# Two weight products by 20 products of blocks instead of 22 in halves

## The chip, the cores and the metric

The kernel runs on one core of one Trainium2 chip. Its time is the device time of one execution in microseconds (us). A core has five engines that run side by side, each with its own instruction stream worked off in order: TensorE (PE, matmuls; PEld is its weight load), VectorE (DVE), ScalarE (ACT), GpSimd (POOL) and SyncE (SP, which here issues the DMAs). They wait for each other through semaphores. Matmuls read SBUF and write PSUM, of which this kernel uses eight banks of 128 x 512 float32; GpSimd works on SBUF alone here.

## The reference

A linear-attention block (RWKV5), with 4 batches, 8 heads, 768 steps and head size 48, feeds a multiplicative feed-forward block on 3072 tokens. The weights `w1`, `w2`, `w3` and `w_out` reach the kernel as float64; all is worked on in float32.

```python
for t in range(S):
    cur = np.einsum('bhd,bhe->bhde', u[None] * kt, vt)
    y[:, :, t] = np.einsum('bhd,bhde->bhe', rt, state + cur)
    state = w[None, :, :, None] * state + np.einsum('bhd,bhe->bhde', kt, vt)
x = np.ascontiguousarray(y.transpose(0, 2, 1, 3)).reshape(B * S, H * D)   # 3072 x 384
a = x @ w1                     # 384 x 1024
b = x @ w2                     # 384 x 1024
out = (a * b @ w3) @ w_out     # 1024 x 1024, 1024 x 384
```

## The kernel before

**Chunks and units.** Time is cut into six chunks (c = 0 to 5) of 128 steps. A unit n is one batch of one chunk, 24 in all; the four units of a chunk give 512 tokens, which stand as `xT[c]`: 128 partitions x 3 blocks of the 384 features x 512 tokens.

**The stages.** First the float64 weights are fetched in 8 + 8 + 16 pieces and converted in place to float32 (words W, M, N or p, H, L, Q; p is a GpSimd instruction, line 396). `w3` is folded with `w_out` into `w34`, 1024 x 384: G turns a row block on VectorE, F multiplies it on TensorE (16 records, line 427), X takes it. F.7 is the last one. Beside this and behind it run the attention of the units (U, A, S, V and others on TensorE; k, d, e, f, x, i, j, m, Y on VectorE; yt turns a unit's output and yx puts it in `xT`), the two products a and b of every chunk, and the products P of a*b with `w34`. Chunk 0 takes a and b by plain matmuls on 512 columns (line 759). The P of a chunk is a seven-product scheme of 2x2 blocks (line 817), two rows of tokens (m = 0, 1) x 7 products x 8 records, with sums s (lines 799, 802) ahead and E (lines 837 to 851) and stores D behind.

**Chunks 1 to 5, a and b.** This is what changes. `product_half` (words pa and pb, lines 912 to 927) takes 2/3 of the features by a seven-product scheme on 2x2 blocks and the last third by plain matmuls: for each weight (a: `w1`, b: `w2`), chunk and half of the output columns (g = 0, 1) there are 8 words, which make 22 matmuls of 128 x 128 weights with 256 token columns. The chip runs a float32 matmul here as two records. They accumulate in four banks: A and F of pool `psF` (4 banks, shared with P, yt and the attention's outputs), B and C of pool `psT` (2 banks, taken once by `ps`, line 897, and kept). `gather_half` (words ga and gb, lines 929 to 953) copies the partial sums between the products with ScalarE, adds with VectorE, and for b multiplies into the tile `abt` of a. The sums of the weights (wa, wb, line 885) and of the tokens (xs, lines 892 to 895) are made by VectorE, the weights' once, the tokens' once in each chunk.

**The order.** Every engine works off its instructions in the order of the list `ORDER`: the function `listed` reads a word such as pa.2.1.4 and calls `product_half("a", 2, 1, 4)`, which issues its instructions on their engines. Nothing reorders them later; semaphores for the data and for the release of buffers are put in for each word. The word Z issues filler matmuls (`busy_array`, line 955). kr, v and W issue loads, y and z the scratch transfers and D the stores, all on SP's queue.

**Buffers that the change touches.** `krin` (the k and r of a unit) has 3 tiles, `abt` 9 of 128 x 2 x 512, the scratch tag `sa` 3 of 128 x 512; the sums s take tiles of their own and, for the other chunks, parts of the weight loads' `raw` tiles.

Of the kernel before, what the change touches and what calls it, by code (L numbers as in the profile page):

```python
# [23 lines left out]
v.1 kr.2 uw k.1 vs.0 ka.0 Z.4.0 T.1 kb.0 T.0 t.1 v.2 U.0 N.0 t.0 R.0 kr.3 ku.0 i.0 j.0 vp.1 U.1 R.1 i.1 r.0 j.1 r.1  # L24
A.0 kr.4 Au.0 k.2 M.0 S.1 S.0 ku.1 m.0 vp.2 R.2 T.2 mo.0 W.1 t.2 H.0 A.1 W.2 r.2 Au.1 fe.0 k.3 L.0 V.0 kr.5 Y.0 m.1
R.3 T.3 ku.2 mo.1 U.2 Q.0 A.2 t.3 Au.2 i.2 r.3 v.3 m.2 yt.0 M.1 mo.2 yx.0 fe.1 ku.3 k.4 Z.3.0 A.3 W.3 V.1 p.2 N.1 R.4
Y.1 v.4 H.1 T.4 M.2 S.2 j.2 kr.6 yt.1 L.1 Au.3 fe.2 H.2 V.2 yx.1 vp.3 Y.2 m.3 a.0.0.0 mo.3 L.2 W.4 yt.2 Q.1 M.3 U.3
W.5 i.3 p.3 t.4 Q.2 b.0.0.0 r.4 v.5 yx.2 k.5 ku.4 a.0.1.0 ub x.5 vp.4 c.0.0.0 A.4 H.3 c.0.1.0 S.3 y.5 ps fe.3 M.4 p.4
u.0.0.0 j.3 L.3 d.5 V.3 W.6 Q.3 M.5 U.4 v.6 Au.4 H.4 p.5 Y.3 kr.8 m.4 yt.3 L.4 b.0.1.0 mo.4 yx.3 i.4 vp.5 a.0.0.1 H.5
W.7 cz.1 a.0.3.2 L.5 Q.4 W.8 M.6 Q.5 p.6 c.0.0.1 vs.6 k.6 b.0.2.2 c.0.3.2 z.5 x.6 H.6 u.0.1.0 M.7 p.7 b.0.4.2 e.5 f.5  # L30
M.8 y.6 h.5 kr.7 L.6 j.4 H.7 S.4 W.9 U.5 L.7 fe.4 Q.6 V.4 l.5 Q.7 p.8 W.10 cz.0 Y.4 A.5 H.8 a.0.2.2 m.5 L.8 W.11 i.5
j.5 M.9 p.9 Q.8 b.0.3.2 k.7 c.0.2.2 z.6 H.9 M.10 p.10 u.0.2.2 L.9 Q.9 a.0.4.2 H.10 u.0.3.2 L.10 W.12 p.11 M.11 Q.10
x.7 a.0.1.1 c.0.4.2 H.11 W.13 L.11 u.0.4.2 U.6 l.6 Q.11 a.0.6.2 k.8 W.14 c.0.1.1 d.6 M.12 p.12 e.6 f.6 v.7 H.12
b.0.0.1 y.7 c.0.6.2 d.7 kr.9 p.13 M.13 e.7 L.12 b.0.1.1 f.7 H.13 Q.12 A.6 M.14 u.0.0.1 p.14 b.0.6.2 L.13 W.15 i.6 vs.7
Q.13 H.14 j.6 L.14 W.16 Q.14 a.0.5.2 u.0.6.2 m.6 W.17 x.8 M.15 p.15 u.0.1.1 a.0.7.2 c.0.5.2 d.8 e.8 z.7 H.15 M.16 p.16
b.0.5.2 L.15 c.0.7.2 Q.15 H.16 W.18 M.17 p.17 L.16 yt.4 Q.16 S.5 yx.4 U.7 g.6 fe.5 W.19 H.17 V.5 b.0.7.2 G.0.0 Y.5
L.17 v.8 u.0.5.2 W.20 l.7 Q.17 p.18 G.0.1 yt.5 M.18 A.7 u.0.7.2 g.7 F.0 i.7 y.8 kr.10 p.19 H.18 j.7 M.19 m.7 L.18 H.19
yx.5 W.21 M.20 Q.18 G.1.0 L.19 p.20 Q.19 vs.8 W.22 U.8 G.1.1 X.0 S.6 H.20 F.1 k.9 L.20 z.8 Q.20 G.2.0 M.21 p.21 x.9
fe.6 H.21 W.23 M.22 p.22 k.10 L.21 V.6 Q.21 X.1 S.7 H.22 W.24 l.8 fe.7 G.2.1 V.7 L.22 Y.7 A.8 W.25 Q.22 yt.7 F.2 G.3.0
yx.7 M.23 p.23 Y.6 i.8 y.9 v.9 j.8 kr.11 M.24 p.24 H.23 m.8 L.23 Q.23 M.25 G.3.1 p.25 yt.6 W.26 X.2 pa.1.0.0 H.24 yx.6  # L40
f.8 L.24 F.3 H.25 ga.1.0.0 Q.24 L.25 W.27 Q.25 g.8 G.4.0 G.4.1 W.28 vs.9 x.10 p.26 M.26 d.9 F.4 z.9 e.9 X.3 f.9 H.26
M.27 p.27 d.10 L.26 e.10 g.9 Q.26 H.27 W.29 p.28 G.5.0 f.10 L.27 Q.27 P.0.0.0 M.28 W.30 X.4 G.5.1 l.9 P.0.1.0 H.28
d.11 L.28 y.10 F.5 e.11 W.31 Q.28 M.29 p.29 G.6.0 f.11 kr.12 H.29 M.30 p.30 v.10 L.29 Q.29 H.30 pa.1.0.1 z.10 X.5
G.6.1 p.31 L.30 M.31 Q.30 F.6 ga.1.0.5 G.7.0 xs.1.0 E.0.0.0 xs.1.1 xs.1.2 kr.13 vs.10 H.31 s.0.1.0 L.31 Q.31 s.0.1.1
# [63 lines left out]
def kernel(  # L108
# [980 lines left out]
```

## Time and profile before

| | |
|---|---|
| median of 3 runs | 500.32 us (497.06, 500.32, 500.47) |
| the profiled execution | 498.53 us |
| its span, first to last instruction | 496.7 us |
| mean granted TensorE clock | 0.988 of full speed |
| F.7 starts, ends | 145.0, 150.4 us |
| last matmul ends | about 490.8 us |
| products of chunks 1 to 5 (lines 922, 926) | 560 + 320 records of 128x256 |

The profile is one execution. A busy time is the time in which an engine had work; matmuls overlap, so the printed duration of one is longer than the step to the next. The slices cut the span in 40 equal parts, with the busy share in tenths. The chain is followed back from the last instruction: at each step to what released it. In a list of instructions the columns are the start, the duration, the engine, the line, what is written and read, its shape and the count; in brackets stands the idle time ahead of it and who ended it. In the table of stages each engine's busy time is followed by its count of instructions, and the last three columns are the granted clock, the share of the DMA engines and GB/s.

### The profile page before, as it was taken

How to read it: one execution, taken by the hardware profiler on the slowest of the kernel's cores; microseconds unless marked ns; L12 is line 12 of the kernel's file. 1: busy time of each engine (PE TensorE's matmuls, PEld its weight loads, DVE VectorE, ACT ScalarE, POOL GpSimd, SP SyncE). 2: the span in 40 equal slices, each digit the busy share in tenths (PEclk: the TensorE clock that was granted, in tenths of full speed). 3: DMA queues.
4: the chain of work that ended last, by engine and by line, in shares of the span. 5: the costliest groups of instructions: out<-in, count | busy, mean ns of one | idle time of the engine just before them, and what ended most of it. 6: DMA issues, size and time to landing. Idle time of an engine off the chain costs nothing.

```text
span 496.7 us, 12176 instructions
## 1 busy us (share of the span) xinstructions
PE 476.6 (96%) x5070; PEld 395.0 (80%) x5070; DVE 328.5 (66%) x647; ACT 197.2 (40%) x454; POOL 62.1 (13%) x57
## 2 busy tenths in 40 slices
PE   8889699999999999999999999999999999999995
PEld 7776445566768988998788898898998889888895
DVE  5879789899999266648694993677472536325152
ACT  3866444857722114008715472332253232122200
POOL 3147354454400000000000000000000000000000
PEclk9989889999999999999999999999999999999999
DMA  8988859899932004325623551034150000100002
GB/s 177 251 230 252 201 163 232 210 215 246 224 72 63 2 16 129 96 65 154 154 78 95 132 127 34 18 112 145 48 148 13 1 3 12 54 1 0 1 1 69
DMA packets 100479, 52.72 MB, mean 106 GB/s; under 512 B 79296, under 2 KB 89792, under 8 KB 100416
## 3 DMA queue, kind: packets, MB, share of 16 engines
q1 hardware_dynamic: 99792, 51.86, 40.5%
q8 instruction: 42, 0.69, 0.6%
q14 instruction: 21, 0.17, 0.1%
q10 hardware_dynamic: 624, 0.00, 0.1%
HBM read 39.65 MB, written 12.19 MB: 104 GB/s over the span
## 4 chain that ended last, share of the span: by engine, by line
PE 82%; DVE 7%; issue 2%; ACT 2%; POOL 2%; DMA 1%; SPq 1%; ACTq 0%; POOLq 0%; DVEq 0%
PE ps_accB L922 10%; PE ps_w L427 6%; PE ps_Ab L922 4%; PE ps_accC L926 3%; PE ps_accC L922 3%; PE ps_a L759 3%; PE ps_s4b L817 3%; PE ps_accB L926 3%; PE ps_a12b L817 3%; PE ps_Aa L922 3%; PE ps_a11b L817 3%; PE ps_s3t L817 3%; PE ps_s1t L817 3%; PE ps_s2t L817 3%; PE ps_a22t L817 3%; PE ps_b L759 3%
## 5 line engine op out<-in xcount | busy, mean ns | idle before, releaser
L396 POOL TENSOR_SCALAR t<-raw 128x512 f32<-128x512 f32 (+2 forms) x30 | 52.4, 1747 | 64.0 <-PE ps_a L570 9.0
L922 PE MATMUL ps_accB<-sumw,w 128*128 128x256 f32 x160 | 45.9, 389 | 0.0
L427 PE MATMUL ps_w<-wo,w3T 128*128 128x384 f32 x128 | 42.7, 488 | 0.0
L427 PEld LDWEIGHTS ps_w<-wo,w3T 128*128 128x128 f32 x128 | 24.0, 190 | 15.5 <-issue 0.2
L471 ACT ACTIVATE ynat<-vnat,dg 128x48 f32<-128x48 f32 x144 | 34.4, 324 | 0.6 <-PE ps_x L729 0.4
L922 PEld LDWEIGHTS ps_accB<-sumw,w 128*128 128x128 f32 x160 | 28.9, 190 | 6.0 <-ACT u2a L939 1.1
L735 ACT COPY xT<-ps_x 128x384 f32<-128x384 f32 x24 | 11.5, 479 | 52.3 <-PE ps_x L729 52.3
L527 ACT COPY kT<-tt 128x1024 f32<-128x1024 f32 x19 | 19.8, 1043 | 24.8 <-PE ps_y L690 18.7
L405 ACT ACTIVATE t<-raw 128x512 uint32<-128x512 uint32 (+2 forms) x32 | 22.6, 706 | 13.4 <-DVE wo L401 5.2
L441 DVE TENSOR_TENSOR krs<-krin,pn_in 128x768 f32<-128x768 f32 (+1 forms) x25 | 23.5, 948 | 5.8 <-PE ps_a L563 4.1
L759 PE MATMUL ps_a<-xT,w 128*128 128x512 f32 (+1 forms) x60 | 24.4, 555 | 0.8 <-ACT xT L735 0.8
L926 PE MATMUL ps_accB<-xT,w 128*128 128x256 f32 x80 | 23.8, 379 | 0.0
L922 PE MATMUL ps_accC<-xT,sumw 128*128 128x256 f32 x80 | 23.8, 379 | 0.0
L926 PE MATMUL ps_accC<-xT,w 128*128 128x256 f32 x80 | 23.8, 379 | 0.0
L922 PE MATMUL ps_Ab<-xT,w 128*128 128x256 f32 x80 | 22.6, 384 | 0.4 <-ACT ps_accB L937 0.4
L759 PE MATMUL ps_b<-xT,w 128*128 128x512 f32 (+1 forms) x60 | 22.2, 512 | 0.5 <-DVE half L609 0.5
L922 PE MATMUL ps_Aa<-xT,w 128*128 128x256 f32 x80 | 22.3, 381 | 0.4 <-ACT ps_accB L937 0.4
L922 PE MATMUL ps_accB<-sumw,sumw 128*128 128x256 f32 x80 | 20.7, 382 | 0.0
L759 PEld LDWEIGHTS ps_a<-xT,w 128*128 128x128 f32 x60 | 11.9, 204 | 10.7 <-issue 8.8
L713 PE MATMUL ps_y<-vodd,AT 64*64 64x48 f32 x384 | 15.6, 222 | 4.4 <-DVE AT L702 3.4
L759 PEld LDWEIGHTS ps_b<-xT,w 128*128 128x128 f32 x60 | 11.1, 191 | 9.6 <-issue 7.9
L570 PE MATMUL ps_a<-kT 64*64 64x64 f32 x768 | 17.1, 226 | 1.6 <-ACT kT L527 0.8
(187 smaller groups left out, 1095.0 us busy)
## 6 DMA issues: line engine op xcount, KB each, us to landing
raw<-in_moe_w_dram SPq DMA_DIRECT2D x64, 128.0 KB, 3.4
scratch<-tr SPq DMA_DIRECT2D x19, 384.0 KB, 3.4
raw<-in_moe_w_dram SPq DMA_DIRECT2D x8, 768.0 KB, 6.2
tt<-scratch SPq DMA_DIRECT2D x38, 128.0 KB, 2.8
krin<-in_k_dram SPq DMA_DIRECT2D x24, 192.0 KB, 4.0
krin<-in_r_dram SPq DMA_DIRECT2D x24, 192.0 KB, 4.1
vnat<-in_v_dram SPq DMA_DIRECT2D x24, 192.0 KB, 3.9
raw<-in_moe_w_out_dram SPq DMA_DIRECT2D x32, 96.0 KB, 2.4
```

Source lines behind the costliest of these rows:

```text
L396: nc.gpsimd.tensor_scalar(part["t", i].bitcast(F32), words(i)[1].bitcast(F32), 0.0, None, ALU.mult)
L405: nc.scalar.activation(out=part["t", i], in_=words(i)[0], func=COPY, scale=2.0 ** -29)
L427: nc.tensor.matmul(ps, lhsT=w3T[j][:, kc, :], rhs=wo[kc], start=(kc == 0), stop=(kc == KF - 1))
L441: nc.vector.tensor_mul(krs[n % NS][:, which, :, :D], kr[:, which], pn[:, which, :, :D])
L471: nc.scalar.activation(out=ynat[n][:, h, :], in_=vnat[n % NV][:, h, :], func=COPY, scale=dg[n][:, h:h + 1])
L527: nc.scalar.copy(out=turned(n).rearrange("x g p (z t) -> x (g p) z t", t=Q), in_=tts.rearrange("x z e t -> x e z t"))
L570: nc.tensor.matmul(upper(n)[rows(a ^ i), i, p, :], lhsT=kT[n][rows(i), p, rows(a)], rhs=rT[n][rows(i), p, rows(a)], start=True, stop=True)
L713: nc.tensor.matmul(yt[n][i][rows(a), p, :], lhsT=AT[n][rows(at), i, p, :], rhs=values, start=not (c or a or p), stop=True, skip_group_chec ...
L759: nc.tensor.matmul(ps, lhsT=(w1 if x == "a" else w2)[:, z, q, js], rhs=xT[c][:, q, ts], start=(q == 0), stop=(q == KM - 1))
L817: nc.tensor.matmul(ps, lhsT=operand(c, j // 2, a)[:, j % 2, m * C:(m + 1) * C], rhs=w34[:, KH * (x == 1) + j, :DH] if x < 2 else made[b][: ...
L922: nc.tensor.matmul(ps, lhsT=quarter(w, g, i, x), rhs=(b11, b21, b22, t4, b12, t2, t3)[x], start=x in (0, 4) and i == 0, stop=True, skip_gr ...
L926: nc.tensor.matmul(ps, lhsT=wide_of[w][:, g + half * HZ, 2, i * P:(i + 1) * P], rhs=xT[c][:, 2, side * TH:(side + 1) * TH], start=False, s ...
```

## The change

For chunks 1 to 5 the scheme of a and b is replaced. The 384 features x 1024 columns of a weight are cut into 3 x 4 blocks, the 384 features x 512 tokens into 3 x 2, and the product is made by 20 products of one block or sum of blocks with another, each with two matmuls on 256 token columns (`product_of_blocks`, words pa.c.x and pb.c.x). Each is added to one of seven accumulators (`INTO`): number 1, 2 and 6 share the two banks of `psT`, number 0, 3, 4 and 7 take a bank of `psF`. `gather_blocks` (ga and gb) reads them out, in mid-accumulation too, with 7 copies on ScalarE (8 for a), 13 instructions on VectorE (14 for b), one addition on GpSimd, and for b seven products by the a side on GpSimd (on VectorE in chunk 5). The sums of the tokens are 3 on VectorE and 10 on GpSimd for each chunk; of the 18 sums of each weight all are on VectorE for `w1`, 5 on VectorE and 13 on GpSimd for `w2`. `krin` has 2 tiles instead of 3, `abt` 8 instead of 9, `sa` 4 instead of 3; the sums s all go to parts of the load tiles. `ps` is gone. The whole list `ORDER` is new; nine Z words with 34 filler matmuls stand in it, for two with 7 before. The counts of all other words are the same. Below, the removed functions are those printed above; of the list the start, the first units, the end of the fold and the head of chunk 5 are shown.

```diff
...
+v.1 v.2 W.1 uw ka.0 k.1 vs.0 Z.2.0 T.0 U.0 t.0 kb.0 R.1 kr.2 ku.0 N.0 R.0 i.0 j.0 r.0 Z.1.1 U.1 vp.1 M.0 kr.3 T.1 i.1
+vp.2 j.1 A.0 t.1 H.0 Au.0 r.1 S.0 ku.1 S.1 m.0 mo.0 W.2 L.0 fe.0 N.1 Z.3.0 A.1 M.1 W.3 Q.0 k.2 ub H.1 Z.6.0 R.2 kr.4
...
+a.0.0.0 M.4 fe.2 W.5 Q.2 p.4 c.0.1.0 V.2 d.5 c.0.0.0 e.5 b.0.0.0 Y.2 v.5 f.5 vp.4 H.4 yt.2 R.4 d.6 yx.2 b.0.1.0 e.6
+L.4 p.6 f.6 M.6 W.7 Q.4 T.4 Au.3 t.4 u.0.0.0 U.3 m.3 ku.4 p.5 i.3 mo.3 Z.1.0 S.3 r.4 j.3 M.5 Z.1.0 A.4 fe.3 k.5 V.3
+vp.5 Au.4 M.7 v.6 cz.1 kr.7 x.5 Y.3 H.5 y.5 H.6 L.5 Q.5 vs.6 Z.10.0 U.4 W.8 yt.3 L.6 m.4 p.7 yx.3 mo.4 W.9 Z.4.0
...
+vs.10 wa.0 wa.9 wa.12 G.7.1 wa.2 F.7 wa.10 X.6 wa.13 wa.14 wa.15 wa.5 wa.6 s.0.0.0 s.0.1.0 wa.1 wa.4 wa.7 wa.8 pa.1.18
+B.0 X.7 xs.1.5 pa.1.15 ga.1.0 xs.1.8 s.0.0.1 pb.1.15 ga.1.1 xs.1.6 ga.1.2 pa.1.2 xs.1.10 B.1 pa.1.8 xs.1.9 s.0.1.1
...
+pa.5.7 gb.4.23 gb.4.22 pb.4.12 Y.22 pb.4.9 gb.4.24 P.4.0.0 gb.4.25 gb.4.26 pb.4.19 E.4.0.0 gb.4.27 s.4.0.0 pb.5.7
+gb.4.28 yt.22 s.4.0.1 P.4.0.1 yx.22 s.4.1.0 xs.5.9 xs.5.3 pa.5.18 s.4.1.1 xs.5.7 s.4.1.3 pa.5.13 ga.5.0 xs.5.5 s.4.0.3
+pa.5.10 s.4.0.2 xs.5.2 P.4.0.2 s.4.1.2 xs.5.11 E.4.0.1 pa.5.15 xs.5.4 E.4.0.2 P.4.0.3 xs.5.6 ga.5.1 ga.5.2 xs.5.12
+pa.5.2 E.4.0.3 xs.5.8 pa.5.8 xs.5.10 pa.5.17 ga.5.4 ga.5.5 pa.5.3 ga.5.10 pa.5.14 ga.5.13 ga.5.7 pa.5.11 ga.5.6
+P.4.0.4 ga.5.8 ga.5.9 pa.5.4 E.4.0.4 ga.5.11 pa.5.20 ga.5.14 pa.5.6 P.4.0.5 ga.5.15 pa.5.5 E.4.0.6 E.4.0.5 P.4.0.6
+D.4.0.0 ga.5.17 pa.5.16 E.4.0.7 D.4.0.1 pb.5.17 ga.5.19 pa.5.1 ga.5.20 ga.5.21 pb.5.15 ga.5.23 pa.5.12 pa.5.9 ga.5.24
...
-    NIN, NV, NS = 3, 3, 2
+    NIN, NV, NS = 2, 3, 2
...
-                abt[c, g] = work.tile([P, 2, NT], F32, tag="abt", bufs=KF + 1, name=f"abt{c}_{g}")
+                abt[c, g] = work.tile([P, 2, NT], F32, tag="abt", bufs=KF, name=f"abt{c}_{g}")
...
-            factor["sa", c, j, part] = a = work.tile([P, NT], F32, tag="sa", bufs=3 if fast else 2, name=f"a{c}_{j}")[:, :ps.shape[1]]
+            factor["sa", c, j, part] = a = work.tile([P, NT], F32, tag="sa", bufs=4 if fast else 2, name=f"a{c}_{j}")[:, :ps.shape[1]]
...
+        split = lambda t: t[:, :NT].rearrange("p (g t) -> p g t", g=2)
+        spare = [split(t.bitcast(F32)[:, x * NT:(x + 1) * NT]) for t in raws for x in range(2 * RAW // NT)] \
+            + [split(t.rearrange("t g h d -> t (g h d)")) for t in (*krin, krs[0])]
...
+                n = 3 if (c, g) == (NCH - 1, 1) else (2 * c + g) % 3
+                s1, s2, s4 = spare[3 * n:3 * n + 3]
...
+                made[nm, c, m] = t = room().tile([P, DH], F32, tag=nm, bufs=1 if fast and nm == "m1" else 2, name=f"{nm}_{c}_{m}")
...
+        NZ = DF // STRIP
+        wide_of = {"a": w1, "b": w2}
+        def block(w, i):
+            return wide_of[w][:, i // KM, i % KM, :]
+        def sums_of_w(w, x):
+            if ("n", w) not in made:
+                tiles = [wide_pool.tile([P, DF], F32, tag="w3", bufs=4, name=f"sumw{2 * (w == 'b') + i}") for i in range(2)]
+                made["n", w] = [t[:, z * STRIP:(z + 1) * STRIP] for t in tiles for z in range(NZ)]
+            n = made["n", w]
+            a = [block(w, i) for i in range(NZ * KM)]
+            out, of, sign, by = ((n[0], a[0], "--", a[10]), (n[1], a[9], "++", a[10]), (n[7], a[0], "++", a[1]),
+                                 (a[1], a[1], "+-", a[10]), (a[9], a[0], "+-", a[9]), (n[4], a[8], "+-", a[11]),
+                                 (a[8], a[7], "+-", a[8]), (n[2], a[8], "++", a[11]), (a[0], a[0], "--", n[2]),
+                                 (n[3], a[6], "--", a[7]), (a[6], a[3], "--", n[3]), (n[4], n[4], "+-", a[6]),
+                                 (a[2], a[2], "+-", a[11]), (n[5], a[6], "+-", a[2]), (n[5], n[5], "+-", a[5]),
+                                 (a[5], a[4], "+-", a[5]), (n[6], a[5], "+-", a[2]), (n[7], n[7], "--", n[6]))[x]
+            if sign == "--":
+                nc.vector.scalar_tensor_tensor(out, of, -1.0, by, ALU.mult, ALU.subtract)
+            else:
+                engine = nc.gpsimd if w == "b" else nc.vector
+                (engine.tensor_add if sign == "++" else engine.tensor_sub)(out, of, by)
+        def wide_side(w, x):
+            n = made.get(("n", w)) or [None] * 8
+            a = lambda i: block(w, i)
+            return {1: n[0], 2: a(10), 3: n[3], 4: a(11), 5: a(8), 6: n[2], 7: n[4], 8: a(6), 9: n[1], 10: n[6], 11: n[5], 12: a(1),
+                    13: a(3), 14: a(7), 15: a(4), 16: a(0), 17: a(2), 18: a(5), 19: a(9), 20: n[7]}[x]
+        def tokens(c):
+            return [xT[c][:, q, x * TH:(x + 1) * TH] for q in range(KM) for x in range(2)]
+        V_AT = (16, 7, 15, 8, 6, 2, 14, 5, 10, 1)
+        def sum_of_tokens(i):
+            if ("v", i) not in made:
+                n = V_AT.index(i)
+                made["v", i] = (work if n < 5 else room()).tile([P, TH], F32, tag=f"x{'wr'[n > 4]}{n % 5}", bufs=1, name=f"x{'wr'[n > 4]}{n % 5}")
+            return made["v", i]
+        def sums_of_x(c, x):
+            b = tokens(c)
+            out, of, add, by = ((16, b[0], 0, b[2]), (7, 16, 0, b[4]), (15, b[3], 1, b[5]), (8, 7, 1, b[1]),
+                                (6, 7, 0, b[5]), (2, b[3], 0, b[1]), (14, 2, 0, 6), (b[0], b[0], 1, b[1]),
+                                (5, b[4], 1, b[5]), (10, b[2], 0, b[5]), (b[4], b[2], 1, b[4]), (b[3], b[2], 1, b[3]),
+                                (1, b[1], 1, b[2]))[x]
+            out, of, by = (sum_of_tokens(t) if isinstance(t, int) else t for t in (out, of, by))
+            engine = nc.vector if x in (0, 1, 3) else nc.gpsimd
+            (engine.tensor_add if add else engine.tensor_sub)(out, of, by)
+        def token_side(c, x):
+            b = tokens(c)
+            plain_or_shared = {18: b[5], 4: b[5], 13: b[1], 9: b[1], 20: b[2], 3: b[0], 19: b[0], 11: b[4], 12: b[3]}
+            return plain_or_shared[x] if x in plain_or_shared else sum_of_tokens(5 if x == 17 else x)
+        INTO = {1: (18, 10, 20, 12), 2: (13, 8, 3, 11), 6: (4, 6, 5, 16, 1, 9, 19), 3: (15,), 4: (7, 14), 0: (17,), 7: (2,)}
+        def product_of_blocks(w, c, x):
+            k = next(k for k, of in INTO.items() if x in of)
+            first = INTO[k][0] == x
+            if first:
+                made["B", w, c, k] = psT.tile([P, NT], F32, tag="t", name=f"ps_acc{k}{w}{c}") if k in (1, 2, 6) \
+                    else psF.tile([P, NT], F32, tag="f", name=f"ps_h{k}{w}{c}")
+            u, ps = wide_side(w, x), made["B", w, c, k]
+            for i in range(2):
+                nc.tensor.matmul(ps[:, i * TH:(i + 1) * TH], lhsT=u[:, i * P:(i + 1) * P], rhs=token_side(c, x),
+                                 start=first and i == 0, stop=True, skip_group_check=True)
+        def gather_blocks(w, c, x):
+            B = lambda k: made["B", w, c, k].rearrange("p (i t) -> p i t", i=2)
+            def out(k):
+                return pair_of(c, k // 2)[:, :, k % 2 * TH:(k % 2 + 1) * TH]
+            def part(k):
+                if w == "a":
+                    return out(k)
+                if ("T", c, k) not in made:
+                    made["T", c, k] = work.tile([P, NT], F32, tag="sa", bufs=4, name=f"T{k}b{c}").rearrange("p (i t) -> p i t", i=2)
+                return made["T", c, k]
+            copies = {0: (3, 1, -1.0), 4: (5, 2, 1.0), 5: (4, 4, 1.0), 8: (2, 2, 1.0), 10: (0, 0, 1.0), 13: (7, 7, 1.0), 19: (1, 6, 1.0)}
+            adds_to = {1: (3, 3), 2: (3, 2), 6: (5, 4), 7: (4, 2), 14: (7, 6), 15: (5, 6), 17: (4, 6), 26: (7, 6)}
+            takes = {9: (2, 1), 21: (0, 1), 23: (7, 6)}
+            by = {3: 3, 12: 2, 16: 5, 18: 4, 22: 0, 25: 1, 27: 7}
+            if x in copies:
+                k, of, scale = copies[x]
+                nc.scalar.activation(out=part(k), in_=B(of), func=COPY, scale=scale)
+            elif x in adds_to:
+                k, of = adds_to[x]
+                nc.vector.tensor_add(part(k), B(of), part(k))
+            elif x in takes:
+                k, of = takes[x]
+                nc.vector.tensor_sub(part(k), part(k), B(of))
+            elif x in by:
+                engine = nc.vector if c == NCH - 1 else nc.gpsimd
+                engine.tensor_mul(out(by[x]), part(by[x]), out(by[x]))
+            elif x == 11:
+                nc.gpsimd.tensor_add(part(2), part(2), part(0))
+            elif x == 20:
+                nc.vector.tensor_add(B(1), B(1), part(1))
+            elif x == 24:
+                nc.vector.tensor_add(part(1), B(1), part(7))
+            elif w == "a":
+                nc.scalar.copy(out=out(6), in_=B(6))
+            else:
+                nc.vector.tensor_mul(out(6), B(6), out(6))
...
```

## The prediction

> **What bounds the kernel now.** I read the page's busy row first, then its slices, the chain, a table of stages, and last the matmuls one by one.
>
> ```profile
> PE 476.6 (96%) x5070; PEld 395.0 (80%) x5070; DVE 328.5 (66%) x647; ACT 197.2 (40%) x454; POOL 62.1 (13%) x57
> ...
> PE   8889699999999999999999999999999999999995
> ...
> DVE  5879789899999266648694993677472536325152
> ...
> POOL 3147354454400000000000000000000000000000
> ...
> PE 82%; DVE 7%; issue 2%; ACT 2%; POOL 2%; DMA 1%; SPq 1%; ACTq 0%; POOLq 0%; DVEq 0%
> ```
>
> TensorE is full from the sixth slice on and carries 82% of the chain. GpSimd is empty after 150 us. Busy time by stage (times, then PE, PEld, DVE, ACT, POOL):
>
> ```profile
> 0.00:75.00 75.00, 64.29 (x1015) 46.26 (x1016) 59.63 (x120) 42.22 (x87) 33.08 (x39) 0.93 0.82 212
> 75.00:150.40 75.40, 74.50 (x637) 46.86 (x636) 69.18 (x126) 45.10 (x100) 29.02 (x19) 1.00 0.85 199
> 150.40:350.00 199.60, 198.12 (x2281) 176.54 (x2281) 137.28 (x272) 73.47 (x182) 0.00 (x0) 1.00 0.33 88
> 350.00:490.80 140.80, 139.70 (x1141) 125.30 (x1139) 62.05 (x129) 36.43 (x85) 0.00 (x0) 1.00 0.09 27
> 490.80:496.70 5.90, 0.00 (x0) 0.00 (x0) 0.36 (x1) 0.00 (x0) 0.00 (x0) 0.88 0.22 72
> ```
>
> 150.4 us is the end of F.7, the last product of the fold. So the span is 150.4 + 340.4 + a tail of 5.9 (the last sum and store), and in the 340.4 TensorE idles 2.6 us. Before 150 us two engines are nearly full: VectorE 69.2 of 75.4, TensorE 74.5.
>
> **TensorE work removed.** The matmul's price is the step from start to start, not the printed duration, since matmuls overlap:
>
> ```profile
> 442.40 0.59 PE L926 MATMUL ps_accB<-xT,w 128*128 128x256 f32 x2
> 442.84 0.59 PE L922 MATMUL ps_accB<-sumw,w 128*128 128x256 f32 x2
> ...
> 476.33 1.46 PE L817 MATMUL ps_s2t<-t,raw 128*128 128x192 f32 x8
> 477.63 1.46 PE L817 MATMUL ps_s4b<-w,raw 128*128 128x192 f32 x8
> ```
>
> Two records, that is one matmul on 256 columns, step by 0.433 us; one product of `P` (8 records) steps by 1.30. Before, one weight and one chunk take 44 such matmuls (2 halves x 22, lines 919 to 927); afterwards 20 products x 2 = 40. Four fewer, 2 weights, 5 chunks: 40 x 0.433 = **17.3 us less**. That is the most that can be won at this bound.
>
> **What of it is kept.** Up to the word F.7 the old list has, of real TensorE work, pa.1.0.0, .1, .4 and .5 (10 matmuls, 4.3 us), P.0.0.0 and P.0.1.0 (2.6) and the U and A of one more unit (1.2) that the new list holds back until later; the new list has only pa.1.13 (0.87) in return. So 7.3 us leave the part ahead of F.7 and are done behind it: 17.3 - 7.3 = 10.0 us less TensorE work after F.7, 337.8 - 10.0 = 327.8. Ahead of F.7 the saving counts only as far as F.7 itself comes earlier. F.7 starts at 145.02, when VectorE's G.7.1 ends (144.14 + 0.70). Between Q.31 and G.7.1 VectorE does 3.0 us of sums now (141.11 to 144.14) and three of 0.41 afterwards, 1.8 less; summed over all words to G.7.1 its rows give 3.1 us less. I take 2: F.7 ends at 148.4. Against it: `NIN` 3 to 2 makes each krin load wait on SP for the readers of the unit two back, not three, with the weight loads, the scratch transfers and v queued behind it, and VectorE has 6 us more listed ahead of unit 3's yx. The 27 more filler matmuls (34 for 7, 0.286 each, 7.7 us) only fill such idle time; TensorE already idles 10.7 us before 75 us. If the first stage slips, F.7 slips: 0 to 8 us.
>
> **VectorE.** Gathering goes from 16 to 27 instructions a chunk (and 7 more in chunk 5, where its products run here): 62 more. Weight sums go from 8 of 128x512 to 23 of 128x256, token sums from 20 to 15. Rows: 0.69 and 0.42 us, so 42.8 + 4.1 - 2.1 = 44.8 us more; back to back they step by 0.60 and 0.41, so about 40 in use. It lies beside TensorE: from F.7 on VectorE would be busy some 240 of 325 us, and some 85% in the stretch to 350 us (137 of 200 now). VectorE reached 24.1 of 25 us from 275 to 300 while TensorE stayed at 24.8, so the load alone is not the bound. ScalarE loses 3 copies a chunk (0.586 each, 8.8 us), off the path.
>
> **The hand-offs.** A bank that is read in mid-accumulation must be read before its next product. There are about 80 such points now (4 in each of 20 halves) and 12 x 10 = 120 afterwards (three in sum 1, two in 2, six in 6, one in 4). Each has one or two products (0.87) listed as cover for one read (0.59 or 0.69). Now TensorE proper loses 0.8 us at them and its weight loads 4.6. Per point that is 0.01 to 0.06 us, so 1 to 7 us; I take **4**.
>
> **GpSimd.** It gets 50 token sums and 13 sums of w2 (128x256) and 38 additions and products (128x512). No row shows a two-input instruction there. From below: the 128x512 memset, 0.53. From above: twice the one-input row, 2 x 1.53 = 3.06. I take 1.53 for 512 columns and 0.8 for 256, nearest to that row, which does the same count of elements: 38 x 1.53 + 63 x 0.8 = 108 us on an engine that is empty. Two places decide whether it reaches TensorE. (1) Ahead of product 6 of w2 in chunks 1, 2 and 4: gb.11 and gb.12 on GpSimd free the buffer for gb.13 (ScalarE, 0.59), then gb.14 (VectorE, 0.69), then pb.6; TensorE has about 4.4 us listed meanwhile (chunk 2: A, pb.20, yt, S, V, S, U). 2 x 1.53 + 1.28 = 4.3 just fits. (2) The head of chunk 5: pa.5.17 needs the ninth GpSimd sum, against six products and two P (7.8 us) and a lead of 0.5: 9 x 0.8 = 7.2 fits.
>
> By the Trainium skill's "GPSIMD Engine Reference", section 3.1, a two-input add of 2048 columns takes 4497 ns there; my estimate from it is 0.56 and 1.12 us, which would leave both places with room.
>
> **The shared port.** VectorE's two-input instructions now run beside GpSimd until 135 us (start, duration; then the other engine):
>
> ```profile
> 116.10 1.54 POOL L396 TENSOR_SCALAR t<-raw 128x512 f32<-128x512 f32 x1 [1.46 <-DVE w3n L408]
> ...
> 110.05 1.52 POOL L396 TENSOR_SCALAR t<-raw 128x512 f32<-128x512 f32 x1 [2.12 <-DVE ynat L722]
> ```
> ```profile
> 116.68 0.65 DVE L401 SCALAR_TENSOR_TENSOR w3n<-w3n,t 128x512 uint32<-128x512 uint32 x1
> ...
> 110.16 1.07 DVE L408 CUSTOM_DVE_ANT_0 w3n<-w3n,t 128x1024 uint16<-128x1024 uint16 x1
> ```
>
> At 116.68 a two-input instruction starts inside a GpSimd one and takes its usual time; at 110.16 it starts just behind one and takes 0.38 longer. From 84 to 140 us four are lengthened, by 1.35 us in all, over 16 GpSimd instructions: 0.08 each. For the 101 after F.7 that is 8 us on an engine with slack; I take **1** for TensorE. Zero is the low end. The high end is a VectorE held for the whole of each GpSimd instruction: some 75 us of those lie before 350 us, VectorE has two SBUF inputs in about 45% of its time by its rows there, and 34 us on top of 85% load makes it the bound, about 10 us.
>
> The skill's "SBUF — State Buffer", section "Who interferes with whom", speaks against this change: a VectorE instruction with two SBUF inputs and a GpSimd one that reads SBUF lock each other out for the whole instruction. The row at 116.68 does not show that; by the rule the sum would be that high end.
>
> **The sum.** 148.4 + 327.8 + 2.6 (idle as now) + 5 (hand-offs 4, port 1) + 5.9 (tail unchanged: the lists end in the same words but for the halves' order) = 489.7 us span. The profiled execution took 498.5 for a span of 496.7, so add 1.8: **491.5 us**, 1.4% under its 498.5. The median shown, 500.3, lies 0.4% over the profiled one, the lowest run 0.3% under; I leave 491.5.
>
> **The rivals.**
> - *All of it is kept.* F.7 ends at 146 and the hand-offs cost nothing: 146 + 327.8 + 2.6 + 5.9 + 1.8 = 484. For it: G.7.1 waits on VectorE, which has less to do there. Against: TensorE is left with filler in the first 75 us.
> - *The gain goes to the start or the port.* F.7 slips by 5, or VectorE is held by GpSimd (10): 491.5 + 5 to 10 = 497 to 502, no change. For it: 6 us more VectorE work ahead of unit 3's yx, krin's two buffers. Against: the row at 116.68.
> - *Slower: GpSimd is late.* Its two-input instructions at the upper end, 3.06 and 1.53. At place (1) TensorE waits 2 x 3.06 + 1.28 - 4.4 = 3 us, three times, 9 us; at the heads 9 x 1.53 - 8.3 = 5.5 in chunk 5 and about 3 in chunks 2 and 3 together. 491.5 + 17.5 = 509. It decides from 1.55 us for 512 columns or 0.92 for 256 on. For it: the fit at 1.53 has no slack and two inputs may cost more than one. Against: the one-input row reads every second word, these read contiguous ones.
> - *The change does not do what it says* is excluded for TensorE: 40 matmuls fewer stand in its instruction order.
>
> **Chances and range.** Forecast (487 to 495) 0.37, all kept 0.17, lost at the start or port 0.20, GpSimd late 0.26. Measured times can tell 1% from no change. Faster by over 1% is the first two less a little at the edge: 0.53; within 1%: 0.20; slower by over 1%: 0.27. The range takes in the kept case and most of the late one: 482 to 510.
>
> **What would show it.** Matmuls of the new products at 128x256, 800 records for 880, still stepping by 0.216. F.7's end near 148. GpSimd's rows for the sums near 0.8 and for the products near 1.5. TensorE's idle from F.7 to the last matmul near 8 us, put down to VectorE and ScalarE reads of the accumulators. If that idle is over 20 us with GpSimd named behind ScalarE's copies or ahead of product 17, the late rival is right; if VectorE's two-input rows grow beyond 0.9 us, the port is. Wrong most easily: GpSimd's price, or the first 75 us, which I read from list positions alone.

## The result, and the profile after

The changed kernel is slower: 515.6 us against 499.5, both medians of four runs (a fourth run of the kernel before, 498.74, moves its median from 500.32), ratio 1.0325 with a 95% interval of [1.027, 1.038]. The forecast was 491.5 and its range ended at 510. The profiled execution took 515.94 us for a span of 514.2.

The page of the kernel after, with rows that were shown of the kernel before (busy times; the slices of VectorE; the chain by engine):

```profile
PE 479.1 (93%) x5042; PEld 385.9 (75%) x5042; DVE 395.6 (77%) x719; ACT 188.2 (37%) x439; POOL 168.1 (33%) x158
...
DVE  6679888889999858886976999976982558654771
...
PE 50%; DVE 30%; ACT 6%; DMA 4%; issue 4%; SPq 2%; POOL 2%; ACTq 0%; DVEq 0%; POOLq 0%
```

TensorE's part of the chain fell from 82% to 50% and VectorE's rose from 7% to 30%, while VectorE is only 77% busy. That is the first sign: VectorE is not full, yet it is what the others wait for. The last product of the fold, F.7, in the list of instructions after:

```profile
143.63 5.40 PE L436 MATMUL ps_w<-wo,w3T 128*128 128x384 f32 x16 [0.95 <-DVE w3T L431]
```

It ends at 149.0. The table of stages, cut there and at the end of the last matmul, 508.3 (times, then PE, PEld, DVE, ACT, POOL):

```profile
75.00:149.00 74.00, 71.08 (x551) 42.10 (x551) 68.40 (x122) 42.83 (x98) 31.35 (x21) 1.00 0.83 199
149.00:350.00 201.00, 189.46 (x2157) 160.55 (x2156) 167.60 (x295) 66.62 (x171) 65.76 (x62) 0.99 0.33 86
350.00:508.30 158.30, 150.50 (x1277) 132.16 (x1276) 99.86 (x179) 35.57 (x85) 40.54 (x36) 1.00 0.10 30
```

The part ahead of F.7 and the tail are as forecast. From F.7 to the last matmul it takes 359.3 us, forecast 335.4: all of the miss, 24 us, is there. In that part TensorE is idle for 19.3 us, and VectorE is busy 267 us where I had put 240. The instructions behind the extra time, line by line (minimum, median and maximum in ns, then first and last start):

```profile
L808 DVE TENSOR_TENSOR raw<-abt,abt x11: 675/684/1743, 146.2 to 491.4; 128x512 f32<-128x512 f32 x11
...
L955 DVE TENSOR_TENSOR abt<-ps_acc6a,abt x20: 650/691/692, 168.7 to 463.4; 128x512 f32<-128x512 f32 x20
...
L914 POOL TENSOR_TENSOR xr<-xT x20: 718/1106/1497, 149.1 to 442.6; 128x256 f32<-128x256 f32 x20
...
L914 DVE TENSOR_TENSOR xw<-xw,xT x10: 424/426/1536, 113.0 to 435.5; 128x256 f32<-128x256 f32 x10
```

VectorE's sums with both inputs in SBUF (808, 914) go up to 1.74 and 1.54 us where they take 0.68 and 0.42 undisturbed. Its sums with one input from PSUM (955) never go over 0.69. GpSimd's sums of 256 columns take 0.72 undisturbed; the row shown has a median of 1.1. Summed by their shapes, VectorE's rows behind F.7 are lengthened by about 25 us.

How this reaches TensorE is seen best at the head of chunk 5, in the list of instructions of all engines:

```profile
434.36 1.21 DVE L808 TENSOR_TENSOR raw<-abt,abt 128x512 f32<-128x512 f32 x1
...
434.98 1.17 POOL L914 TENSOR_TENSOR xT<-xT 128x256 f32<-128x256 f32 x1
435.49 0.95 DVE L914 TENSOR_TENSOR xw<-xw,xT 128x256 f32<-128x256 f32 x1
...
436.36 1.21 DVE L811 TENSOR_TENSOR raw<-raw,abt 128x512 f32<-128x512 f32 x1
...
436.98 1.17 POOL L914 TENSOR_TENSOR xw<-xT 128x256 f32<-128x256 f32 x1
...
437.60 2.23 DVE L811 TENSOR_TENSOR raw<-abt,raw 128x512 f32<-128x512 f32 x2
438.23 1.06 POOL L914 TENSOR_TENSOR xT<-xT 128x256 f32<-128x256 f32 x1
...
439.76 2.33 DVE L811 TENSOR_TENSOR abt<-abt 128x512 f32<-128x512 f32 x2
...
442.01 0.35 DVE L843 TENSOR_TENSOR osb_top<-ps_a12b,m 128x192 f32<-128x192 f32 x1
...
442.51 1.10 PE L932 MATMUL ps_h3a<-xw,w 128*128 128x256 f32 x4 [3.62 <-DVE osb_top L843]
```

The instructions of both engines are lengthened here. The instruction at 442.01 (E.4.0.1) reads the bank of P.4.0.1 and so frees it for product 15 of w1, which is TensorE's next work. It stands in VectorE's order behind seven sums that begin at 434.36. They should step by 0.60 and 0.41, 4.0 us; they take 7.65. The difference, 3.6 us, is TensorE's wait in the bracket (3.62). GpSimd's sum that product 15 reads (436.98) was done at 438.15. The list of waits also puts 3.9 us of the weight load for product 15 down to a GpSimd sum (the one that starts at 440.49, 1.05 long), but that ended at 441.54 and VectorE's read at 442.36, and the weights came at 442.48. So GpSimd's own lateness did not decide here.

### The profile page after: what moved, and what is told of

Its sections match the earlier page's. It is cut to its first block, busy times and chain, and to the rows that moved or that the text cites. A ratio compares the mean times of both kernels' runs of the same rounds, so it can differ in the third digit from the quotient of the medians.

```text
span 514.2 us, 12355 instructions
## 1 busy us (share of the span) xinstructions
PE 479.1 (93%) x5042; PEld 385.9 (75%) x5042; DVE 395.6 (77%) x719; ACT 188.2 (37%) x439; POOL 168.1 (33%) x158
## 4 chain that ended last, share of the span: by engine, by line
PE 50%; DVE 30%; ACT 6%; DMA 4%; issue 4%; SPq 2%; POOL 2%; ACTq 0%; DVEq 0%; POOLq 0%
PE ps_acc6a L932 5%; PE ps_acc6b L932 4%; DMA raw<-in_moe_w_dram 3%; PE ps_acc2b L932 3%; PE ps_s4b L826 3%; PE ps_a22t L826 3%; PE ps_acc1b L932 3%; PE ps_s1t L826 3%; DVE raw L811 3%; PE ps_s2t L826 2%; PE ps_s3t L826 2%; DVE ruk L459 2%; DVE abt L955 2%; PE ps_a12b L826 2%; DVE raw L808 2%
## 5 line engine op out<-in xcount | busy, mean ns | idle before, releaser
L914 POOL TENSOR_TENSOR xr<-xT 128x256 f32<-128x256 f32 x20 | 20.9, 1050 | 36.0 <-ACT xT L744 25.4
L630 DVE COPY_PREDICATED AT<-later,ps_a 128x512 f32<-128x512 int32 x24 | 17.5, 730 | 9.4 <-PE ps_a L600 6.8
L963 POOL TENSOR_TENSOR T2b<-T2b,T0b 128x512 f32<-128x512 f32 x5 | 6.6, 1324 | 46.7 <-DVE T2b L958 35.1
L699 PE MATMUL ps_y<-half,kT 64*64 64x48 f32 x384 | 15.8, 221 | 5.8 <-DVE half L624 2.1
L955 DVE TENSOR_TENSOR abt<-ps_acc6a,abt 128x512 f32<-128x512 f32 x20 | 13.7, 686 | 8.3 <-PE ps_acc6a L932 5.3
L826 PE MATMUL ps_s2t<-t,raw 128*128 128x192 f32 x88 | 17.4, 341 | 2.0 <-DVE raw L811 2.0
L520 DVE STREAM_TRANSPOSE tr<-krs 128x768 f32<-128x768 f32 x19 | 18.3, 964 | 1.2 <-DMA scratch<-tr 1.1
L744 ACT COPY xT<-ps_x 128x384 f32<-128x384 f32 x24 | 11.3, 476 | 21.6 <-PE ps_x L738 21.6
L826 PE MATMUL ps_a22t<-t,abt 128*128 128x192 f32 x96 | 17.7, 328 | 1.2 <-DVE u L845 1.2
L826 PE MATMUL ps_a11b<-w,abt 128*128 128x192 f32 x96 | 18.8, 341 | 0.0
L826 PE MATMUL ps_a12b<-w,abt 128*128 128x192 f32 x96 | 17.9, 328 | 0.1
```

The source lines that it names most:

```text
L520: nc.vector.transpose(out=blocks[n].rearrange("x m e t -> x e m t"), in_=krs[n % NS][:, :, :, :D])
L826: nc.tensor.matmul(ps, lhsT=operand(c, j // 2, a)[:, j % 2, m * C:(m + 1) * C], rhs=w34[:, KH * (x == 1) + j, :DH] if x < 2 else made[b][: ...
L914: (engine.tensor_add if add else engine.tensor_sub)(out, of, by)
L955: nc.vector.tensor_add(part(k), B(of), part(k))
```

## The experiments

The theories: *port*, a GpSimd instruction that reads SBUF holds VectorE's instructions that have two SBUF inputs, and the held VectorE holds TensorE. *Load*, the 62 added gathers are too much for VectorE by themselves. *Late*, GpSimd's results come too late for TensorE, as in the rival of the prediction.

**GpSimd reads nothing.** In the kernel after, each two-input operation of GpSimd becomes one column (of each half, where there are two) and two memsets of the rest. By its rows that takes about 0.92 us for a sum and 1.25 for a product, where the undisturbed operations take 0.72 and 1.27; order, waits and all other engines stay. The sums and products of a and b that GpSimd makes are so left out of what is computed.

```diff
+        def as_long(op, out, of, by):
+            op(out[..., 0:1], of[..., 0:1], by[..., 0:1])
+            for _ in range(2):
+                nc.gpsimd.memset(out[..., 1:], 0.5)
...
-                nc.gpsimd.tensor_add(part(2), part(2), part(0))
+                as_long(nc.gpsimd.tensor_add, part(2), part(2), part(0))
```

> GpSimd's two-input sums and products of chunks 1 to 5 become a one-column sum or product and two memsets of the rest: about as long as the two-input rows at their shortest (0.72 and 1.27 us), after the same waits, but they read almost nothing. The values of a and b are left wrong by it. Theory 'port' (a VectorE instruction with two SBUF inputs and a two-input GpSimd one exclude each other): VectorE's lengthened rows (about 25 us behind F.7) go back to 0.42 and 0.69, and the time falls from 515.6 to 490 to 498. Theory 'load' (VectorE's 62 more gathering instructions and the 120 hand-offs are the loss): 511 to 517, since VectorE's instructions are the same. Theory 'late' (TensorE waits for the length of GpSimd's chains): 509 to 517, since GpSimd's instructions are as long.

Measured: 492.64 us, 0.990 of before [0.986, 0.994]. Its busy row and chain, and its stages from the end of its F.7 on:

```profile
PE 471.1 (96%) x5042; PEld 382.9 (78%) x5042; DVE 367.8 (75%) x719; ACT 187.9 (38%) x439; POOL 156.6 (32%) x360
...
PE 76%; DMA 7%; DVE 7%; ACT 4%; SPq 3%; issue 2%; POOL 0%; ACTq 0%; DVEq 0%; POOLq 0%
```
```profile
145.80:350.00 204.20, 201.90 (x2394) 173.91 (x2395) 162.82 (x323) 75.42 (x197) 68.75 (x213) 1.00 0.35 92
350.00:484.10 134.10, 132.30 (x1043) 117.26 (x1044) 78.47 (x152) 26.71 (x59) 25.76 (x82) 1.00 0.07 24
```

VectorE has the same 719 instructions and all added gathers, GpSimd is busy nearly as long (94.5 us behind F.7, for 106.3 with its lengthened rows), and 23 us are gone, with VectorE's share of the chain back at 7%. TensorE's idle time behind F.7 is 4.1 us, for 19.3 in the kernel after. Load and late both fall as causes of the 23 us: the same VectorE instructions and nearly the same GpSimd times do not cost them when GpSimd does not read. Of the 24.2 us between the two spans, 21.0 lie behind F.7 (338.3 against 359.3) and 3.2 ahead of it. The 3.2 can be chance: in the profiled executions of the kernel before and of the last three changes of it in this section, alike up to 220 us, F.7 starts between 142.0 and 145.3.

**Work moved to VectorE.** Three kernels give work of GpSimd to VectorE in place, in the kernel after: all of it; the 63 sums alone; the 38 products and additions alone.

```diff
-                engine = nc.gpsimd if w == "b" else nc.vector
+                engine = nc.vector
...
-            engine = nc.vector if x in (0, 1, 3) else nc.gpsimd
+            engine = nc.vector
...
-                engine = nc.vector if c == NCH - 1 else nc.gpsimd
+                engine = nc.vector
...
-                nc.gpsimd.tensor_add(part(2), part(2), part(0))
+                nc.vector.tensor_add(part(2), part(2), part(0))
```

(All four edits; the first two for the sums; the last two for the products.)

> All 63 sums and 38 products and additions of GpSimd go to VectorE, in the same list. Nothing runs on GpSimd behind F.7. VectorE loses the 25 us of lengthening and gets 63 x 0.41 + 38 x 0.60 = 49 us. 'Port': about 24 us more on VectorE in all, spread, 510 to 525; no row of a two-input instruction over 0.75 (512 columns). 'Load': VectorE is the bound, so its 49 us go to the end: 540 or more. 'Late': GpSimd's chains become shorter (0.42 for 0.72 and more), so under 510.

> Only the 50 token sums and 13 sums of w2 go to VectorE; the products and additions stay on GpSimd. 'Port': the sums stand where VectorE makes its own two-input sums (149 to 170 us and the heads of the chunks), some 16 of the 25 us of lengthening; VectorE gets 26 us of them. On balance 505 to 515. 'Load': 520 or more. 'Late': 505 or less, as the heads no longer wait on GpSimd.

> Only the 28 products and 10 additions of 512 columns go to VectorE; the sums stay on GpSimd. 'Port': VectorE gets 23 us and loses some 9 us of lengthening: 515 to 523. 'Load': 528 or more. 'Late': 513 to 516, the heads being untouched.

Measured: 513.03 [ratio 1.025, 1.034], 514.25 [1.028, 1.036] and 519.28 [1.040, 1.048], each within what port expected and outside load. The busy time of VectorE tells why it hardly matters where this work is done: 408.4, 397.2 and 406.4 us, for 395.6 in the kernel after. The 63 sums are 63 x 0.42 = 26 us of VectorE's own work; on GpSimd they relieve it by 1.6 us. The 38 others are 38 x 0.69 = 26 us, and relieve it by 10.8. VectorE's own work is not free here either: against the kernel whose GpSimd reads nothing, these three have 40.6, 29.4 and 38.6 us more on VectorE and take 20.4, 21.6 and 26.6 us longer. So load fails as the cause of the loss, since VectorE is not full and its time does not reach the end one for one; but half of it or more does.

**Only the sums, or only the products, read nothing.** The first edit, applied to one of the two groups; that group is left out of what is computed.

```diff
-                (engine.tensor_add if sign == "++" else engine.tensor_sub)(out, of, by)
+                as_long(op, out, of, by) if w == "b" else op(out, of, by)
...
+                as_long(nc.gpsimd.tensor_add if add else nc.gpsimd.tensor_sub, out, of, by)
```
```diff
+                    as_long(engine.tensor_mul, out(by[x]), part(by[x]), out(by[x]))
...
+                as_long(nc.gpsimd.tensor_add, part(2), part(2), part(0))
```

> The kernel after with GpSimd's 63 sums (128x256) each replaced by a one-column operation and two memsets, so it reads nothing there for long; the 38 products and additions stay on GpSimd as they are. The sums of the tokens and of w2 are left out of what is computed. 'Port': the VectorE rows that were lengthened stood mostly beside sums (some 16 of 25 us), so most of the 23 us comes back: 498 to 504. 'Load': nothing comes back, 513 to 517. 'Late': only the heads of the chunks come back (pa.17 no longer late), 510 to 513.

> The kernel after with GpSimd's 38 products and additions (128x512) each replaced by a one-column operation and two memsets; the 63 sums stay as they are. These products and additions of a and b are left out of what is computed. With the sums made blind it took 499, with both 493, so by 'port' the products alone should give back about a third of the 23 us, if the two parts add up: 506 to 511. 'Late': the chain ahead of product 6 of w2 is the main loss, 500 to 506. 'Load': 513 to 517.

Measured: 499.23 [ratio 0.998, 1.006] without the sums' reads, 502.54 [1.005, 1.020] without the products'. The first is as port expected, the second came back further than I had put it, into the bracket that I had given to late. So the parts do not add up: 16.4 and 13.1 us for 23.0 together. VectorE's busy time falls by 16.9 and by 12.2 us of 27.8, which nearly adds up; it is the price to TensorE that falls faster than VectorE's time. A reading that fits, and that no run shows by itself: the first microseconds taken off VectorE are those that TensorE waited for. That late is not hidden in the second run follows from the first kernel, where the products keep nearly their length and all of their places, and all is gained.

**The prices by themselves.** A small kernel runs VectorE and GpSimd on tiles of 128x512, alone and side by side, stage by stage:

```diff
+        stages = ((v_two, 10, None, 0), (None, 0, g_two, 6), (None, 0, g_one, 6), (v_two, 12, g_two, 6), (v_psum, 12, g_two, 6),
+                  (v_two, 14, g_one, 6), (v_two, 14, g_step, 6), (v_two, 8, g_set, 8), (v_scaled, 16, g_two, 6))
```

> Nothing of the reference is computed here: nine stages behind one another, each with a hand-off ahead of it, measure the disputed cost by itself on 128x512 float32 tiles. VectorE alone with two SBUF inputs; GpSimd alone with two, then with one input; VectorE with two SBUF inputs beside GpSimd with two; VectorE with one PSUM and one SBUF input beside GpSimd with two; VectorE with two beside GpSimd with one input; the same with GpSimd reading every second word; VectorE with two beside GpSimd memsets; VectorE with one SBUF input beside GpSimd with two. 'Port': alone 0.69 and 1.27 us; in the fourth stage each VectorE row shows about 0.69 + 1.2 us of the other engine at its worst, the two engines in turn, and the stage lasts about the sum of both (6 x 1.27 + 12 x 0.69 = 16 us); in the fifth, with PSUM, both go at their own pace; memsets hinder nothing. If one input on GpSimd locks as well, the sixth and seventh stages lengthen too; by the reading in the prediction they do not. 'Load': the fourth stage lasts as long as its longer engine alone (8.3 us) and no row grows. 'Late': the same as load, GpSimd's two-input row at 1.5 us or more.

Its rows by line, in the order of the stages (line 31 VectorE with two SBUF inputs, 32 with PSUM and SBUF, 33 with one; 34 GpSimd with two, 35 and 36 with one, 37 its memset):

```profile
L31 DVE TENSOR_TENSOR vc<-va,vb x10: 684/692/693, 3.0 to 9.5; 128x512 f32<-128x512 f32 x10
...
L34 POOL TENSOR_TENSOR gc<-ga,gb x6: 1262/1262/1262, 10.7 to 17.4; 128x512 f32<-128x512 f32 x6
...
L31 DVE TENSOR_TENSOR vc<-va,vb x12: 682/1162/1635, 28.6 to 42.2; 128x512 f32<-128x512 f32 x12
L34 POOL TENSOR_TENSOR gc<-ga,gb x6: 1588/1590/1717, 29.4 to 37.9; 128x512 f32<-128x512 f32 x6
...
L32 DVE TENSOR_TENSOR vc<-ps,vb x12: 690/691/693, 43.0 to 51.0; 128x512 f32<-128x512 f32 x12
L34 POOL TENSOR_TENSOR gc<-ga,gb x6: 1265/1267/1270, 43.3 to 50.1; 128x512 f32<-128x512 f32 x6
...
L31 DVE TENSOR_TENSOR vc<-va,vb x14: 692/693/979, 51.7 to 62.8; 128x512 f32<-128x512 f32 x14
L35 POOL TENSOR_SCALAR gc<-ga x6: 1657/1658/1942, 52.5 to 61.5; 128x512 f32<-128x512 f32 x6
...
L33 DVE TENSOR_SCALAR vc<-va x16: 426/427/1369, 81.4 to 94.0; 128x512 f32<-128x512 f32 x16
```

Two inputs against two: both engines lengthen. VectorE's twelve take 13.9 us in all for 8.3 alone, so each GpSimd instruction costs VectorE 0.93 us and itself 0.33. The stage lasts 14.2 us; strictly in turn would be 6 x 1.27 + 12 x 0.69 = 15.9, free of each other 8.3. So the hold is most of a GpSimd instruction (0.93 of 1.27), not all of it. With one input from PSUM nothing is lengthened on either side. Against GpSimd's one-input instruction VectorE's fourteen lose 1.7 us, 0.29 for each GpSimd instruction; reading every second word changes that little (maximum 1.00), and beside memsets the rows stay at 0.69. This is the distinction that my reading of the kernel before could not see: its GpSimd rows had one input at most.

**The cause put into the kernel before.** First, 80 GpSimd instructions behind the gathered parts of a and b, reading those parts, with two inputs (the same part twice) and with one:

```diff
+            if x > 3 and (x < 8 if w == "a" else x > 4):
+                of = {5: at(0, 0), 6: at(0, 1), 7: at(1, 0)}.get(x, at(1, 1))
+                nc.gpsimd.tensor_add(spare[8 if c % 2 else 2], of, of)
```
```diff
+                nc.gpsimd.tensor_scalar(spare[8 if c % 2 else 2], of, 0.5, None, ALU.mult)
```

> The cause alone, put into the kernel before: 80 additions of 128x512 with two SBUF inputs on GpSimd, each behind a gathered part of a or b, into a tile that nothing reads. TensorE's and VectorE's lists are those of before, and GpSimd was empty there. 'Port': about 100 us of GpSimd work lock the VectorE rows with two SBUF inputs (the s sums, the rows of the scan, the sums of the tokens); fewer stand beside it than in the kernel after, since most gathers read PSUM: 502 to 510 against 498. 'Load' and 'late': nothing waits for these additions but the next write of the same part, and no VectorE instruction is added: 497 to 500.

> As the kernel before with 80 GpSimd instructions, but each with one SBUF input (a multiplication by a constant) in place of the addition: same places, same waits. The prediction took one-input rows as the price of the lock. 'Port, only with two inputs': 497 to 500, clearly under the run with the additions. 'Port, with any input read from SBUF': about the time of the run with the additions. 'Late' (the waits for GpSimd behind the gathered parts cost, not the lock): also the time of the run with the additions, but with VectorE's rows at 0.69.

Measured: 513.12 [ratio 1.023, 1.033] and 508.04 [1.015, 1.023]. Both are above what I had expected by port, and the second fits none of the three as I put them. The reason is in the list of who waited for these instructions. VectorE waited 12.9 us for the first kind (8.0 to write a part that GpSimd still read, 4.9 to write the tile that I had taken for scratch) and 9.8 us for the second. The two runs mix two causes. So a second pair, and a control, work in place on a tile that nobody writes next:

```diff
+            if c > 1 and x > 3 and (w == "b" and x > 4 or w == "a" and x < 8 and (c, g) != (3, 0)):
+                own, by = (spare[8], spare[7]) if c % 2 == 0 else (spare[2], spare[1])
+                for _ in range(2):
+                    nc.gpsimd.tensor_sub(own, own, by)
```
```diff
+                    nc.gpsimd.tensor_scalar(own, own, 1.0, None, ALU.mult)
```
```diff
+                    nc.gpsimd.memset(own, 0.5)
```

> The last two runs mixed the lock with waits for GpSimd (the next writer of a part waited until GpSimd had read it). Here 120 GpSimd subtractions of 128x512 with two SBUF inputs are put into the kernel before at the same kind of place (chunks 2 to 5, two behind each gathered part), in place on a tile that is dead there, so that nobody waits for them. 'Port': by the stage measured alone each costs VectorE up to 0.93 us where VectorE has two SBUF inputs; about half of VectorE's time after 165 us is such work, so its busy time grows by 25 to 45 us and the time to 508 to 522. 'Load': VectorE's list is that of before, 497 to 500. 'Late': the waits were the whole cost of the last two runs, so 497 to 500 as well.

> The same 120 places and the same dead tile, with one SBUF input (a multiplication by 1) in place of the subtraction. 'Port': by the stage measured alone 0.29 us each beside such VectorE work, so a third of the other's loss: 500 to 507, VectorE 8 to 18 us busier. If the size of my one-input price (0.08 us each) was right: 498 to 500. 'Load' and 'late': 497 to 500.

> The control: the same 120 places and the same tile, with memsets, which read nothing. All theories: 497 to 500, VectorE as busy as in the kernel before. Anything above 501 says that the mere presence of GpSimd instructions in these places costs time, and the two runs beside it would have to be read against this one.

The tile was not dead everywhere: P.2.0.6 still reads a sum of chunk 2 there, so with the subtraction and the memset that one product has other values.

Measured: 527.44 us with two inputs, ratio 1.060 [1.054, 1.066]; 501.55 with one, 1.010 [1.006, 1.013]; 497.77 with memsets, 1.000 [0.997, 1.003]. By the lists of line 957, no instruction waited for GpSimd in any of the three. Its rows, in this order of kernels:

```profile
L957 POOL TENSOR_TENSOR raw<-raw x120: 1260/1272/1921, 224.9 to 495.8; 128x512 f32<-128x512 f32 x120
```
```profile
L957 POOL TENSOR_SCALAR raw<-raw x120: 1487/1488/2258, 223.3 to 479.4; 128x512 f32<-128x512 f32 x120
```
```profile
L957 POOL MEMSET raw<- x120: 525/525/527, 221.6 to 444.7; 128x512 f32 x120
```

The one-input instructions occupy GpSimd longer and cost 4 us; the two-input ones cost 30. That is above what I had put by port (508 to 522), though VectorE's lengthening is inside it: more of it came through to TensorE than I had allowed. With one input the time is inside and the lengthening, 6.4 us, just under. What happens on VectorE beside the two-input ones, first the row of line 895 in the kernel before, then VectorE's list of instructions beside them:

```profile
L895 DVE TENSOR_TENSOR sumw<-xT,sumw x5: 417/424/425, 141.7 to 435.6; 128x256 f32<-128x256 f32 x5
```
```profile
236.74 1.37 DVE L895 TENSOR_TENSOR sumw<-xT,sumw 128x256 f32<-128x256 f32 x1
...
239.69 1.51 DVE L453 TENSOR_TENSOR ruk<-ruk,ub 128x384 f32<-128x384 f32 x1
241.30 0.55 DVE L457 TENSOR_REDUCE dg<-ruk 128x8 f32<-128x384 f32 x1
...
245.50 0.69 DVE L941 TENSOR_TENSOR ps_accC<-ps_Fa,u2a 128x512 f32<-128x512 f32 x1
```

A sum of 256 columns, 0.42 otherwise, takes 1.37: it is held for 0.95 us, three quarters of an undisturbed GpSimd instruction (1.27). The product of line 453, 0.56 otherwise, takes 1.51. The reduction with one input (0.55) and the addition from PSUM (0.69) beside them are not touched.

**What a held VectorE costs**, from the profiled busy times of VectorE and the median times:

| kernel, against | VectorE busy | VectorE more | time more |
|---|---|---|---|
| before with one-input reads, against before (328.5) | 334.9 | 6.4 | 4.0 |
| before with two-input reads, against before | 367.0 | 38.5 | 29.9 |
| after without the sums' reads, against after without any (367.8) | 378.7 | 10.9 | 6.6 |
| after without the products' reads, against the same | 383.4 | 15.6 | 9.9 |
| after, against the same | 395.6 | 27.8 | 23.0 |

Between 0.6 and 0.8 of each microsecond by which VectorE is held comes through to the time. Two things blur the figures. Beside these runs the kernel before had medians of 497.5 to 499.5 us, so a difference of two medians is uncertain by some 2 us. And the profiled execution with two-input reads had a mean granted TensorE clock of 0.974, for 0.988 in the kernel before; 1.4% of its span of 525.8 us is about 7 us (an estimate of the most), so in that row up to a quarter of the 29.9 can be TensorE's slower clock. What lowered it is not shown. No kernel that makes all of the sums and products in the new scheme ran faster than the kernel before.

## Why the prediction was wrong, by its own steps

- **The bound and TensorE's saving** held. With GpSimd's reads gone the time is 492.64 where the sum gave 491.5, and F.7 to the last matmul takes 338.3 us where work, idle time, hand-offs and port were put at 335.4. That the times agree to 1.1 us is in part luck: F.7 ended 2.6 us earlier than put, and the part behind it took 2.9 longer. In the kernel after, the new matmuls step as the old ones did (product 18 of w1 starts at 148.87, the next at 149.73, 0.86 for four records), so the 17.3 us of work are saved; what GpSimd's reads cost is more.
- **What is kept of it, F.7 at 148.4**: it ended at 149.0 after, 145.8 without the reads. They differ by no more than F.7 moves from one execution of a list to another (3.3 us, above), so the fewer `krin` tiles and the filler cost nothing that shows, and the 2 us taken for VectorE's lighter load cannot be told either.
- **VectorE's added work**: 44.8 us were put; without the reads VectorE is 39.3 us busier than before (the "about 40 in use" of the prediction). That this load alone is not the bound was right.
- **The hand-offs at 4 us** were put too low. Without GpSimd's reads there is no port to pay, and the 338.3 above less the work (327.8) and the idle time of before (2.6) leaves 7.9 us for them and all else, just over the 1 to 7 given. By the lists of waits, the weight loads of the new products then wait 11.6 us for VectorE and ScalarE, where those of the old ones waited 4.6. They were not measured by themselves.
- **GpSimd's price**: 1.27 and 0.72 us undisturbed, where I took 1.53 and 0.8; its busy time rose by 106 us, lengthened rows included, where I had 108: the lengthening made up for a price put too high. The estimate from the Trainium skill's "GPSIMD Engine Reference", section 3.1, 1.12 and 0.56 by proportion from 2048 columns, was 0.15 us low for both lengths.
- **The shared port, the step that failed.** I took 1 us for TensorE, between 0 and about 10; it is 23 (21 behind F.7). It failed twice. First, the kind of row: the price 0.08 us for each GpSimd instruction was read from rows with one input. For that kind it was even fair (6.4 us over 120 instructions is 0.05), but two inputs cost VectorE 38.5 / 120 = 0.32 in the same places. The Trainium skill's "SBUF — State Buffer", section "Who interferes with whom", says that one waits for the whole instruction of the other; the 1.37 us row and the probe show most of that, 0.95 and 0.93 of 1.27 us, and I let the row at 116.68 outvote it. The probe tells why that row could look as it did: beside one-input GpSimd instructions the typical VectorE row is 0.693 us, and only some are lengthened, to at most 1.00. The page does not set GpSimd's one-input operations apart; by the runs they cost VectorE about a third as much or less.
- Second, **the way from VectorE to TensorE**. Even my high end, 34 us on VectorE, was turned into 10 by setting it against VectorE's idle time over the whole stage. VectorE lost 28, fewer than that, and TensorE 23. An average load of 85% says nothing of the head of chunk 5, where one read that frees a bank stands behind seven sums, and there the whole lengthening, 3.6 us, is TensorE's wait.
- **The rivals.** "All kept" (484) and "late" (509) did not come. Places (1) and (2) of late did not decide: no wait of TensorE's matmuls in the kernel after is put down to GpSimd; of its weight loads' waits 6.2 us are, 3.9 of them in the place above where VectorE's read ended later. Of the chain's pieces behind F.7 four are GpSimd's, 5.1 us in all. The sums at the head of chunk 5 did pass the 0.92 us from which I had let it decide (six of the ten, at 1.05 to 1.17 us), against 0.72 undisturbed: they were held themselves. The rival "the gain goes to the port" named the mechanism and was priced at 497 to 502, by the same division through the slack.
- **What would show it** was put rightly: VectorE's two-input rows beyond 0.9 us mean the port. They went to 1.7. TensorE's idle time from F.7 on, put near 8 us, was 19.3.

## What to carry to other kernels

Before handing elementwise work from VectorE to GpSimd, count what VectorE will do meanwhile with two SBUF inputs: here 63 sums moved away relieved VectorE of 1.6 us instead of 26; the rest came back as held instructions. A row is evidence for an instruction of its own kind only; one input does not price two. And VectorE's slack must be looked up where a read that frees a bank stands behind other work, not averaged over a stage: of each microsecond that VectorE was held, 0.6 to 0.8 reached the end.

## What the runs showed of the hardware beyond that

The probe's last stage shows the same hold for a VectorE instruction with one SBUF input: its multiplication by a constant takes 0.427 us undisturbed, 0.78 in the mean and 1.37 at most beside GpSimd's two-input additions. So "two inputs" is not the whole condition on VectorE's side, while the reduction in the list above, also with one input, was not held. The Trainium skill's "SBUF — State Buffer", section "Who interferes with whom", names both cases: a multiplication of this kind can enter a mode that takes the shared pair of ports, a reduction on this chip can't. The trace agrees with both outcomes; it shows who is held beside whom, not the mode or the ports. A GpSimd memset beside VectorE's two-input additions, 0.525 us in every case, was not lengthened and lengthened nothing.
